# Third exp part of VectorE's pairs multiplied with a scaled copy of V, the second norm in the first norm's buffers, pairs in the first chunk

## The chip, the cores and the metric

One core of a Trainium2 chip runs the whole kernel. Its engines have instruction queues of their own: TensorE (PE, with the loads of its weights as PEld), VectorE (DVE), ScalarE (ACT), GpSimd (POOL) and SyncE (SP), which here only starts DMAs. The metric is the device time of one launch in microseconds, the median of several runs. Beside it stands one execution taken by the hardware profiler; the times of single instructions come from that one.

## The reference

Two identical layers over 2048 rows of 512 values in bf16. Each is an attention block with 32 heads of 16 values, then a dense block with 1792 hidden values and a relu, both behind a norm without weights and with a residual. Both layers use the same weights.

```
x = A_x
x = x + attention(layernorm(x), wqkv, wo)
x = x + relu(layernorm(x) @ w1) @ w2
x = x + attention(layernorm(x), wqkv, wo)
x = x + relu(layernorm(x) @ w1) @ w2

attention: q, k, v = split(x @ wqkv)         # 32 heads of 16
           p = softmax(q @ k.T / 4)           # 2048 x 2048 for each head
           return (p @ v) @ wo
```

The exps of the softmax are the bulk of the work: 2 layers × 32 heads × 2048 × 2048 values.

## The kernel before

**Units, segments, slots.** A unit is the scores of one head for 128 keys (a key block, kb 0 to 15) and 512 query rows. There are 4096 such blocks. A segment (`sg`) is what is summed in one go in `ps_o`: four heads (g 0 to 3, all even or all odd in one group T of eight heads), one chunk of queries (l, j) and a list of key blocks; with all 16 it has 64 units. In layer 1 the queries from row 1024 on are cut in four chunks of 256 rows, and there a unit holds two key blocks of half the width. In the first chunks of a layer segments are split over parts of the key blocks, because K and V are still being made, and their sums are kept in buffers (`acc0`, `acc`) that have other uses later; the eighth of `acc0` is the tile `xn2T`.

The main loop (L1150) runs slot by slot. A slot takes three units, computes their scores into three PSUM banks (L1250; the same matmuls are repeated when PE has time to spare), and takes the exp with one ScalarE activation over 1536 columns (L1259). The products with V (`pv`, L883) follow some slots later; four heads' products run side by side as one round.

**Pairs.** In some slots the third unit goes to VectorE instead, and the activation has only 1024 columns. Two such blocks, taken two slots apart, make a pair. For each block `first_step` (L980) writes `lin`, an integer from which bf16 bits follow that approximate the exp linearly. When the second is there, `chain` (L1015) does five operations over both blocks, 1024 columns: it takes the mantissa out of `lin` (L1020), squares it (L1028), multiplies it by CUBE = 0.1667 (L1029), takes the power of two into `step` (L1020 once more), and multiplies the squared mantissa with `lin` into `cube` (L1032). The exp is the sum of `lin`, `step` and `cube`. Nobody adds them: each of the three is multiplied with V by a matmul of its own, so that a block of a pair costs three products and another block one. V carries two columns of ones, so the softmax's denominators come out of the same products.

**When a pair starts.** The condition at L1173 to L1193 asks that fewer than NP = 4 pairs are under way, that all V of layer 0 is there (`("v", 0, 15) in made`), in layer 1 that K is complete or the pace low, that VectorE's planned work is at most BACKLOG = 6000 ns ahead, and that the pair will be ready before its segment (or one of the next two) ends. NC = 3 buffers exist for `step` and `cube`.

**The order of everything is written out in advance.** The kernel is built by a small planner with clocks of its own for PE and VectorE (`now_pe`, `now_dve`). VectorE's tasks lie in `dve_q` with costs and dependencies; `run_dve` emits those that are due, evacuations of `ps_f` first. PE's other work (projections, transposes, output projection, dense block) lies in `work` as groups of matmuls and is filled in between scores and products, so much for each slot as the pace at L1221 says: what is left, divided by the slots left of the chunk, with some slots added or taken off. `run_until` forces what the next unit needs. So a change of costs or conditions changes the order of all engines' work.

**Norms and buffers.** The first norm of a chunk is transposed into `xnT[j]`, from which Q, K and V are made. The second norm, ahead of the dense block, is transposed into the one tile `xn2T` (L725), which waits (`war_x`) until the H matmuls of an earlier chunk have read it. `h_group` (L653) reads it. At the end of the kernel, L1354 and L1363 use it too.

Of the kernel before, what the change touches and what calls it, by code (L numbers as in the profile page):

```python
# [24 lines left out]
def kernel(  # L25
# [44 lines left out]
    NP = 4  # L70
    NC = 3

    MM = 216.0
# [25 lines left out]
    def sb(shape, dt, name):  # L99
# [11 lines left out]
    kt2 = [sb([P, 2, QS], BF16, f"ktp0_2_{n}") for n in range(2)]  # L111
    kt3 = [sb([P, QS], BF16, f"ktp_{T}_3") for T in range(4)]
    ktp = [
        [[kt01[T][:, 0, :], kt01[T][:, 1, :], kt2[T // 2][:, T % 2, :], kt3[T]] for T in range(4)],
        [
            [sb([P, QS], BF16, f"ktp1_{T}_{j}") for j in range(NQS - 1)] + [kt3[T]]
            for T in range(4)
# [8 lines left out]
        [sb([P, H // 2, PW], BF16, f"vaug1_{kb}") for kb in range(NKB - TPC)] + vaug[0][NKB - TPC :]  # L126
    )
    xnT = [sb([P, NDC, QS], BF16, f"xnT{j}") for j in range(NQS)]
    xn2T = sb([P, NDC, QS], BF16, "xn2T")
    htp = [sb([P, 2, QS], BF16, f"ht{n}") for n in range(NF // 2)]  # L130
# [11 lines left out]
    acc0 = [x[:].bitcast(FP32).rearrange("p a b -> p (a b)") for x in htp]  # L142
    acc0.append(xn2T[:, 0:2, :].bitcast(FP32).rearrange("p a b -> p (a b)"))
    ebuf = [sb([P, W * QS], BF16, f"e{n}") for n in range(NE)]
# [448 lines left out]
    def v_in(b):  # L593
        return b.rearrange("p (h e d) -> p h e d", e=2, d=DH)

    def v_group(l, kb):
        def fin(b):
            nc.vector.tensor_copy(out=v_out(l, kb), in_=v_in(b))
            mark(("v", l, kb))

        return mm_group(v_mms(kb), fin, [("v", l, kb)], each(TPC, "xnT", ("ln1", l, kb // TPC)))
# [51 lines left out]
    def h_group(l, j, ft, war):  # L653
        n = (l * NQS + j) * NF + ft
        _, a, w = columns(l, j)

        number = QS // w
        fts = range(ft, ft + number)
        made_here = [("h", l, j, f) for f in fts]

        def fin(b):
            out = htp[ft // 2][:, ft % 2 : ft % 2 + number, a : a + w]
            sums = b.rearrange("p (f q) -> p f q", f=number)
            if ending[0]:
                nc.scalar.activation(out=out, in_=sums, func=ACTF.Relu)
            else:
                nc.vector.tensor_scalar(  # L667
                    out=out, in0=sums, scalar1=0.0, scalar2=None, op0=ALU.max
                )
            for key in made_here:  # L670
                mark(key)

        def after():
            for f in range(number):
                load_w1(n + f + NW1)

        return mm_group(
            [
                (w1buf[(n + f) % NW1][:, c, :], xn2T[:, c, a : a + w])
                for f in range(number) for c in range(NDC)  # L680
            ],
            fin, made_here,
            each(w // P, "xnT", ("ln2", l, j)) + war + [("w1", n + f) for f in range(number)],
            after=after, wide_by=w, sums=number,
        )
# [32 lines left out]
    def rest_of_chunk(l, j):  # L718
# [4 lines left out]
        war_h = each(chunks[b][1], "z", *b) if b else []  # L723
        war_x = each(NF, "h", *b) if b else []
        work[0:0] = [o_group(l, j, i) for i in range(n)] + ln_groups(  # L725
            ("ln2", l, j), xn2T, a, n, war_x
        )
# [154 lines left out]

    def pv(sg, kb, g, rhs):  # L883
        e = sg["e"]
        sg["rem"][g] -= 1
        nc.tensor.matmul(  # L886
            ps_o[32 * g : 32 * g + 32, 0 : sg["w"]],
            vaug[sg["l"]][kb][:, 4 * sg["T"] + g, 2 * e : 2 * e + 32],
            rhs, start=g not in sg["begun"], stop=not sg["rem"][g],
# [28 lines left out]
    def v_round(found, t):  # L918
        pe_run("v", 1, t)
        sg = segs[seg_at[0]]  # L920
        for n in range(QS // sg["w"]):
            for g in range(4):
                of_g = [f for f in found if f[1][2] == g][n : n + 1]
                for home, x, rhs in of_g:
                    home[:] = [y for y in home if y is not x]
                    pv(sg, x[1], g, rhs)
        while pend and not pend[0]["blocks"]:
# [48 lines left out]
    def dve_block(half, taken, src, ex, recent):  # L976
# [20 lines left out]
        if half == 0:  # L997
            pair_no[0] += 1
            pairs.append({"sg": taken[0][0], "key": ("e", pair_no[0]), "n": pair_no[0], "blocks": [], "mms": []})
# [5 lines left out]
        p["mms"] += [  # L1005
            (sg, kb, g, part[:, half * QS + n * sg["w"] : half * QS + (n + 1) * sg["w"]].bitcast(BF16), key)
            for part, key in (
                (lin[which], line_key), (step[p["n"] % NC], p["key"] + (3,)), (cube[p["n"] % NC], p["key"])
# [6 lines left out]
    def chain(p):  # L1015
# [3 lines left out]
        def bits(keep, put):  # L1019
# [4 lines left out]

        mantissa = stair.bitcast(BF16)
        steps = (
            (342, lambda: bits(0x7F, 0x3F80)),
# [6 lines left out]
        )  # L1034
        for n, (cost, fn) in enumerate(steps):
            k = key + (n,) if n + 1 < len(steps) else key
            early = [("added", p["n"] - NC)] if p["n"] > NC else []
            task(cost, fn, [k], [key + (n - 1,)] if n else early)
            maker[k]["chain"] = p
# [75 lines left out]
    for sg in segs:  # L1115
        both = QS // sg["w"]
        for kbs in zip(*[iter(sg["kbs"])] * both):
            units.extend(tuple((sg, kb, g) for kb in kbs) for g in range(4))
# [17 lines left out]

    wide[0] = False
    seen = set()
    level = 0.0
# [10 lines left out]
    while units:  # L1150
# [15 lines left out]


        half = None
        if len(banked) == W and pair_at in (None, no):
            mine = banked[-1][0][0]  # L1170
            if pair_at == no:
                half, take = 1, pairs[-1]["sg"]
            elif (not pairs or pair_no[0] + 1 - pairs[0]["n"] < NP) and ((mine['l'] or ("v", 0, 15) in made) and (not mine['l'] or ('k', 1, 0, NQS - 1) in made or pace < PAIR_PACE)):  # L1173
                queued = sum(t["cost"] for t in dve_q if "chain" in t)
# [19 lines left out]
            if half is not None:  # L1194
                other = [pairs[-1]["blocks"][0][0][2]] if half else []
                of_take = [x for x in banked if x[0][0] is take]
                if of_take:
                    x = next((x for x in of_take[::-1] if x[0][2] not in other), of_take[-1])
                    banked.remove(x)
                else:  # L1200
                    units.appendleft(banked.pop())
                    x = take_unit(heads(banked) + other, take)
                    for sg, kb, g in x:
                        run_until(("k", sg["l"], sg["T"], kb // TPC))
# [13 lines left out]
        if first["l"] and first["early"]:  # L1218
            rest = sum(x[0][0]["early"] for x in itertools.islice(units, 400)) / W - 20.0
        pace = (  # L1220
            3.0 if first["short"] and not first["l"] else max(todo / max(rest + (0.0 if first["j"] == NQS - 1 and not first["l"] else AHEAD[first["l"]] if first["j"] < (LAST if first["l"] else NQS - 1) else -6.0), 6.0), 0.5)  # L1221
        )
# [194 lines left out]
```

The softmax here doesn't subtract the row's maximum and nothing guards it: scores larger than these inputs give would overflow.

## Time and profile before

| what | value |
|---|---|
| runs shown, median of 8 | 1626.31 us (1624.83 to 1633.44) |
| profiled execution | 1630.59 us |
| its span | 1628.8 us |
| granted TensorE clock, mean | 0.992 |
| score blocks on VectorE | 612 (306 pairs) |
| slots (activations at L1259) | 1366 |

The span is the profiled execution from its first instruction to its last; 1.8 us of its time lie around it. Rows of groups give: line, engine, operation, out <- in, shapes, count, then busy time and mean ns of one, then the idle time of the engine just before them with what ended most of it. The mean is from an instruction's start to its end, and on ScalarE and VectorE one instruction can begin before the one ahead of it has ended. In a list in order of time the first number is the start and the second the length, both in us.

In 40 equal slices of the span, in tenths of the slice, the engines were busy as follows (41 us a slice):

```
PE   8899889999999999999999998889989999999997
DVE  7458999999999999999899999999999999999994
ACT  6999999999999999999999999999999999999994
PEclk9997999999999999999999999999999999999999
```

### The profile page before, as it was taken

To read this page: it belongs to the slowest core of one execution; us is meant where nothing else is said; L and a number is where in the kernel's file an instruction comes from. 1 tells how busy PE (TensorE), PEld (TensorE's weight loads), DVE (VectorE), ACT (ScalarE), POOL (GpSimd) and SP (SyncE) were. 2 spreads that over 40 slices of the span, in tenths; PEclk is the share of its full clock that TensorE was granted. 3 is DMA by queue.
4 is the path that set the end of the run, shared out by engine and by line. 5 is a ranking of instruction groups with operands and counts; after the bars stand their busy time and mean duration, and the time that the engine had idled before them with its cause. 6 is when DMAs were issued, how large, how long until landed. Compare 5 with 4: busy or idle time off the path is not lost.

```text
span 1628.8 us, 35297 instructions
## 1 busy us (share of the span) xinstructions
PE 1491.9 (92%) x14728; PEld 504.7 (31%) x14728; DVE 1507.9 (93%) x3133; ACT 1586.0 (97%) x1385; POOL 96.3 (6%) x279
## 2 busy tenths in 40 slices
PE   8899889999999999999999998889989999999997
PEld 3222222222222222222222222222233333344344
DVE  7458999999999999999899999999999999999994
ACT  6999999999999999999999999999999999999994
POOL 2000001000010010100100000001000110010100
PEclk9997999999999999999999999999999999999999
DMA  5000000210001100111000100000210111112121
GB/s 162 1 1 2 2 2 8 44 28 11 8 15 41 27 14 3 21 41 21 15 1 16 32 1 1 2 3 8 50 26 16 32 27 34 35 39 54 26 61 49
DMA packets 113889, 39.96 MB, mean 25 GB/s; under 512 B 103328, under 2 KB 111264, under 8 KB 113728
## 3 DMA queue, kind: packets, MB, share of 16 engines
q1 hardware_dynamic: 101696, 26.21, 7.0%
q0 software_dynamic: 10688, 10.18, 3.3%
q8 instruction: 115, 1.88, 0.5%
q10 hardware_dynamic: 1344, 1.31, 0.2%
q14 instruction: 46, 0.38, 0.1%
HBM read 24.38 MB, written 2.10 MB: 16 GB/s over the span
## 4 chain that ended last, share of the span: by engine, by line
ACT 81%; PE 9%; DVE 7%; issue 2%; DMA 0%; ACTq 0%; DVEq 0%
ACT e L1259 81%; PE ps_s L1250 3%; PE ps_o L886 2%; PE ps_f L429 2%; DVE lin L980 2%; DVE step L1020 1%; PE ps_s L1313 1%; DVE cube L1032 1%; DVE cube L1028 1%; DVE cube L1029 0%; DVE stats L460 0%; DVE q L610 0%; DVE ht L667 0%; DVE u L809 0%; DVE xn L502 0%
## 5 line engine op out<-in xcount | busy, mean ns | idle before, releaser
L1259 ACT ACTIVATE e<-ps_s 128x1536 bf16<-128x1536 f32 (+1 forms) x1366 | 1576.1, 1403 | 8.4 <-PE ps_s L1250 7.9
L1250 PE MATMUL ps_s<-q,ktp 32*128 32x512 bf16 (+1 forms) x6053 | 603.0, 343 | 91.3 <-ACT e L1259 77.6
L886 PE MATMUL ps_o<-e,vaug 128*32 128x512 bf16 (+1 forms) x4348 | 514.6, 347 | 14.5 <-DVE u L809 5.9
L980 DVE TENSOR_SCALAR lin<-ps_s 128x512 int16<-128x512 f32 x612 | 416.2, 684 | 27.0 <-PE ps_s L1250 22.0
L1250 PEld LDWEIGHTS <-ktp 32*128 32x128 bf16 x6053 | 185.2, 91 | 506.9 <-issue 384.7
L886 PEld LDWEIGHTS <-vaug 128*32 128x32 bf16 x6664 | 166.5, 94 | 349.1 <-issue 337.8
L1020 DVE TENSOR_SCALAR step<-lin 128x1024 int16<-128x1024 int16 x612 | 241.7, 417 | 0.4
L1028 DVE TENSOR_TENSOR cube<-step 128x1024 f16<-128x1024 bf16 x306 | 208.2, 681 | 1.4
L1032 DVE TENSOR_TENSOR cube<-cube,lin 128x1024 bf16<-128x1024 f16 x306 | 207.3, 677 | 0.0
L886 PE MATMUL ps_o<-cube,vaug 128*32 128x512 bf16 (+1 forms) x772 | 147.8, 343 | 0.0
L886 PE MATMUL ps_o<-step,vaug 128*32 128x512 bf16 (+1 forms) x772 | 147.2, 343 | 0.0
L429 PE MATMUL ps_f<-xn2T,w 128*128 128x512 bf16 (+1 forms) x504 | 130.1, 347 | 6.2 <-DVE ht L667 3.3
L886 PE MATMUL ps_o<-lin,vaug 128*32 128x512 bf16 (+1 forms) x772 | 126.6, 340 | 4.3 <-DVE u L809 2.6
L1029 DVE TENSOR_SCALAR cube<-cube 128x1024 f16<-128x1024 f16 x306 | 127.2, 416 | 1.4
L429 PE MATMUL ps_f<-w,ht 128*128 128x512 bf16 x406 | 125.1, 384 | 1.2 <-DVE x L693 0.9
L836 POOL DMA_DIRECT2D r<-u x52 | 38.4, 739 | 1191.7 <-DVE lin L980 605.3
L429 PE MATMUL ps_f<-xnT,wqkv 128*128 128x512 bf16 (+1 forms) x328 | 91.3, 364 | 3.0 <-DVE xnT L553 0.5
L429 PE MATMUL ps_f<-wo,ot 128*128 128x512 bf16 x240 | 74.1, 384 | 1.9 <-DVE x L633 0.7
L610 DVE TENSOR_SCALAR q<-ps_f,qmask 128x512 bf16<-128x512 f32 (+1 forms) x102 | 64.8, 658 | 9.9 <-PE ps_f L429 9.6
L667 DVE TENSOR_SCALAR ht<-ps_f 128x512 bf16<-128x512 f32 x105 | 71.8, 683 | 1.8 <-PE ps_f L429 1.4
L429 PEld LDWEIGHTS <-w 128*128 128x128 bf16 x504 | 39.3, 97 | 64.4 <-issue 55.7
L822 DVE SCALAR_TENSOR_TENSOR ot<-u,mask,r 128x512 bf16<-128x512 f32 (+2 forms) x82 | 51.0, 624 | 1.1
(86 smaller groups left out, 587.4 us busy)
## 6 DMA issues: line engine op xcount, KB each, us to landing
w<-in_B_w_dram SPq DMA_DIRECT2D x140, 128.0 KB
r<-u POOLq DMA_DIRECT2D x25, 256.0 KB, 7.1
r<-u POOLq DMA_DIRECT2D x27, 128.0 KB, 4.6
out_dram<-x SPq DMA_DIRECT2D x16, 128.0 KB
x<-in_A_x_dram SPq DMA_DIRECT2D x14, 128.0 KB
w<-in_B_w_dram SPq DMA_DIRECT2D x1, 1792.0 KB
wqkv<-in_A_wqkv_dram ACTq DMA_DIRECT2D x2, 512.0 KB
c<-u SPq DMA_DIRECT2D x48, 8.0 KB
```

Of the source, the lines that this page charges most:

```text
L429: nc.tensor.matmul(out, lhsT, rhs, start=i % k == 0, stop=i % k == k - 1)
L610: return nc.vector.tensor_scalar(out=qbuf[n % 2][e][:, 0:w], in0=b, scalar1=qmask[e][:, 0:1], scalar2=None, op0=ALU.mult,)
L667: nc.vector.tensor_scalar(out=out, in0=sums, scalar1=0.0, scalar2=None, op0=ALU.max)
L822: nc.vector.scalar_tensor_tensor(out=ot[t][:, at_column + a : at_column + a + w], in0=u[:, a : a + w], scalar=mask[e][:, 0:1], in1=r[:, a ...
L886: nc.tensor.matmul(ps_o[32 * g : 32 * g + 32, 0 : sg["w"]], vaug[sg["l"]][kb][:, 4 * sg["T"] + g, 2 * e : 2 * e + 32], rhs, start=g not in ...
L980: first = nc.vector.tensor_scalar(out=lin[which][:, half * QS : (half + 1) * QS], in0=src, scalar1=EXP_BIAS, scalar2=0.0, op0=ALU.add, op1 ...
L1020: nc.vector.tensor_scalar(out=stair, in0=line, scalar1=keep, scalar2=put, op0=ALU.bitwise_and, op1=ALU.bitwise_or,)
L1028: (609, lambda: nc.vector.tensor_mul(out=power, in0=mantissa, in1=mantissa)),
L1029: (342, lambda: nc.vector.tensor_scalar(out=power, in0=power, scalar1=CUBE, scalar2=None, op0=ALU.mult)),
L1032: (609, lambda: nc.vector.tensor_mul(out=power.bitcast(BF16), in0=power, in1=line.bitcast(BF16))),
L1250: nc.tensor.matmul(b[:, a : a + sg["w"]], kt[32 * g : 32 * g + 32, kc : kc + P], qbuf[sg["n"] % 2][sg["e"]][32 * g : 32 * g + 32, 0 : sg[" ...
L1259: ex = nc.scalar.activation(out=eb[:, 0 : place[m]], in_=b[:, 0 : place[m]], func=ACTF.Exp, scale=1.0 / (LOG2E * UNIT),)
```

## The change

Three things are changed.

1. **A scaled copy of V.** For the key blocks 8 to 11 a second copy of V, `vthird`, holds V times CUBE, the columns of ones included. When both blocks of a pair have such key blocks and the copies are there, the pair leaves out the multiply by CUBE and its `cube` part is multiplied with `vthird`; otherwise it stays as it was. The copies are made on VectorE, once in each layer; in layer 1 they wait for the pairs that still read layer 0's copies. Full segments take these key blocks last, and when a unit is picked for a pair, one with such a key block is looked for in the slot and then further on in the segment.
2. **The second norm goes into the first norm's buffers**: `xnT[j]` in place of `xn2T`, which is gone. The wait `war_x` is gone with it. The eighth of `acc0` is now a tile `kt1`, which holds two tiles of layer 1's K later.
3. **Pairs in the first chunk**, before all V is made: one at a time, from the second K tile of the first group of heads on. And the last chunk of layer 0 plans its other work for 8 slots fewer than it has.

```diff
+    THIRD = (8, 9, 10, 11)
...
+    kt1 = sb([P, 2, QS], BF16, "ktp1_0")
...
-            [sb([P, QS], BF16, f"ktp1_{T}_{j}") for j in range(NQS - 1)] + [kt3[T]]
+            [
+                kt1[:, j, :] if T == 0 and j < 2 else sb([P, QS], BF16, f"ktp1_{T}_{j}")
+                for j in range(NQS - 1)
+            ] + [kt3[T]]
...
+    vthird = {kb: sb([P, H // 2, PW], BF16, f"vthird_{kb}") for kb in THIRD}
-    xn2T = sb([P, NDC, QS], BF16, "xn2T")
...
-    acc0.append(xn2T[:, 0:2, :].bitcast(FP32).rearrange("p a b -> p (a b)"))
+    acc0.append(kt1[:].bitcast(FP32).rearrange("p a b -> p (a b)"))
...
+    def scale_v(l, kb, deps):
+        task(
+            225, lambda: nc.vector.tensor_scalar(
+                out=vthird[kb][:], in0=vaug[l][kb][:], scalar1=CUBE, scalar2=None, op0=ALU.mult
+            ),
+            [("third", l, kb)], [("v", l, kb)] + deps,
+        )
...
     def v_group(l, kb):
         def fin(b):
             nc.vector.tensor_copy(out=v_out(l, kb), in_=v_in(b))
             mark(("v", l, kb))
+            if l == 0 and kb in THIRD:
+                scale_v(l, kb, [])
...
-                (w1buf[(n + f) % NW1][:, c, :], xn2T[:, c, a : a + w])
+                (w1buf[(n + f) % NW1][:, c, :], xnT[xj][:, c, a : a + w])
...
-        war_x = each(NF, "h", *b) if b else []
         work[0:0] = [o_group(l, j, i) for i in range(n)] + ln_groups(
-            ("ln2", l, j), xn2T, a, n, war_x
+            ("ln2", l, j), xnT[xj], a, n, []
         )
...
-    def pv(sg, kb, g, rhs):
+    def pv(sg, kb, g, rhs, p=None):
         e = sg["e"]
+        values = vthird[kb] if p and p["scaled"] else vaug[sg["l"]][kb]
...
-            vaug[sg["l"]][kb][:, 4 * sg["T"] + g, 2 * e : 2 * e + 32],
+            values[:, 4 * sg["T"] + g, 2 * e : 2 * e + 32],
...
+        p["scaled"] = all(
+            ("third", sg["l"], kb) in made for us in p["blocks"] for sg, kb, g in us
+        )
...
-        for n, (cost, fn) in enumerate(steps):
+        nos = (0, 1, 3, 4) if p["scaled"] else range(5)
+        for n, after in zip(nos, (None,) + tuple(nos)):
+            cost, fn = steps[n]
...
-        for kbs in zip(*[iter(sg["kbs"])] * both):
+        order = sorted(sg["kbs"], key=lambda kb: len(sg["kbs"]) == NKB and kb in THIRD)
+        for kbs in zip(*[iter(order)] * both):
...
+        if banked[0][0][0]["l"] and not scaled_two[0]:
+            scaled_two[0] = True
+            for kb in THIRD:
+                scale_v(1, kb, [("added", p["n"]) for p in pairs])
...
-            elif (not pairs or pair_no[0] + 1 - pairs[0]["n"] < NP) and ((mine['l'] or ("v", 0, 15) in made) and (not mine['l'] or ('k', 1, 0, NQS - 1) in made or pace < PAIR_PACE)):
+            elif (not pairs or pair_no[0] + 1 - pairs[0]["n"] < NP) and ((mine['l'] or ("v", 0, 15) in made or not pairs and ("k", 0, 0, 1) in made) and (not mine['l'] or ('k', 1, 0, NQS - 1) in made or pace < PAIR_PACE)):
...
-                if of_take:
-                    x = next((x for x in of_take[::-1] if x[0][2] not in other), of_take[-1])
+                third = half == 0 or all(y[1] in THIRD for y in pairs[-1]["blocks"][0])
+                fit = next(
+                    (
+                        x for x in of_take[::-1]
+                        if third and x[0][2] not in other
+                        and all(("third", y[0]["l"], y[1]) in made for y in x)
+                    ), None
+                )
+                far = None
+                if third and not fit:
+                    far = next(
+                        (
+                            x for x in units if x[0][0] is take
+                            and x[0][2] not in heads(banked[:-1]) + other
+                            and all(
+                                ("third", y[0]["l"], y[1]) in made
+                                and ("k", y[0]["l"], y[0]["T"], y[1] // TPC) in made for y in x
+                            )
+                        ), None
+                    )
+                if far:
+                    units.remove(far)
+                    units.appendleft(banked.pop())
+                    x = far
+                elif fit or of_take:
+                    x = fit or next((x for x in of_take[::-1] if x[0][2] not in other), of_take[-1])
...
-            3.0 if first["short"] and not first["l"] else max(todo / max(rest + (0.0 if first["j"] == NQS - 1 and not first["l"] else AHEAD[first["l"]] if first["j"] < (LAST if first["l"] else NQS - 1) else -6.0), 6.0), 0.5)
+            3.0 if first["short"] and not first["l"] else max(todo / max(rest + (-8.0 if first["j"] == NQS - 1 and not first["l"] else AHEAD[first["l"]] if first["j"] < (LAST if first["l"] else NQS - 1) else -6.0), 6.0), 0.5)
...
-        uses(copy(out=xn2T[:, :, part(i)], in_=pt), more[i], "xnT")
+        uses(copy(out=xnT[NQS - 1][:, :, part(i)], in_=pt), more[i], "xnT")
...
-                    b, w1buf[n % NW1][:, c, :], xn2T[:, c, at_column : at_column + width],
+                    b, w1buf[n % NW1][:, c, :], xnT[NQS - 1][:, c, at_column : at_column + width],
```

More of the change, by code (lines that the diff above doesn't have):

```diff
@@ L654, in h_group @@
         n = (l * NQS + j) * NF + ft
-        _, a, w = columns(l, j)
+        xj, a, w = columns(l, j)
         number = QS // w
@@ L925, in v_round @@
                     home[:] = [y for y in home if y is not x]
-                    pv(sg, x[1], g, rhs)
+                    pv(sg, x[1], g, rhs, *x[5:])
         while pend and not pend[0]["blocks"]:
@@ L998, in dve_block @@
             pair_no[0] += 1
-            pairs.append({"sg": taken[0][0], "key": ("e", pair_no[0]), "n": pair_no[0], "blocks": [], "mms": []})
+            pairs.append({"sg": taken[0][0], "key": ("e", pair_no[0]), "n": pair_no[0], "blocks": [], "mms": [], "scaled": False})
         p = pairs[-1]
@@ L1006, in dve_block @@
             (sg, kb, g, part[:, half * QS + n * sg["w"] : half * QS + (n + 1) * sg["w"]].bitcast(BF16), key)
+            + ((p,) if key == p["key"] else ())
             for part, key in (
@@ L1034, in chain @@
         )
-        for n, (cost, fn) in enumerate(steps):
+        nos = (0, 1, 3, 4) if p["scaled"] else range(5)
+        for n, after in zip(nos, (None,) + tuple(nos)):
+            cost, fn = steps[n]
             k = key + (n,) if n + 1 < len(steps) else key
             early = [("added", p["n"] - NC)] if p["n"] > NC else []
-            task(cost, fn, [k], [key + (n - 1,)] if n else early)
+            task(cost, fn, [k], [key + (after,)] if n else early)
             maker[k]["chain"] = p
@@ L1137 @@
     wide[0] = False
+    scaled_two = [False]
     seen = set()
@@ L1202 @@
                     x = take_unit(heads(banked) + other, take)
+                if True:
                     for sg, kb, g in x:
```

## The prediction

> **What bounds the kernel now.** I read the table of engines first: ACT 97%, DVE 93%, PE 92%. An average names no bound, so the groups by line and shape come next, then engine time by stage, then DVE in order of time.
>
> ```profile
> PE 1491.9 (92%) x14728; PEld 504.7 (31%) x14728; DVE 1507.9 (93%) x3133; ACT 1586.0 (97%) x1385; POOL 96.3 (6%) x279
> ...
> ACT 81%; PE 9%; DVE 7%; issue 2%; DMA 0%; ACTq 0%; DVEq 0%
> ...
> L1259 ACT ACTIVATE e<-ps_s 128x1536 bf16<-128x1536 f32 x753 | 1121.1, 1597 | 4.9 <-PE ps_s L1250 4.6
> L1259 ACT ACTIVATE e<-ps_s 128x1024 bf16<-128x1024 f32 x612 | 673.5, 1164 | 3.5 <-PE ps_s L1250 3.3
> ...
> L1029 DVE TENSOR_SCALAR cube<-cube 128x1024 f16<-128x1024 f16 x306 | 127.2, 416 | 1.4
> ```
>
> ACT waits 8.4 us in all before its exps (4.9 + 3.5) and carries 81% of the chain of waits: the time is the sum of ACT's exps. A slot with a VectorE block has an exp of 1024 columns instead of 1536: 1597 − 1164 = 0.433 us less. So **one block on VectorE takes 0.433 us off the end, a pair 0.866 us.** How many pairs there are (306 now) is a question to VectorE:
>
> ```profile
> 42.00:110.00 68.00, 60.49 (x445) 20.08 (x442) 27.39 (x47) 68.00 (x52) 0.00 (x0) 1.00 0.00 1
> 110.00:161.00 51.00, 47.22 (x337) 12.12 (x336) 43.55 (x86) 47.29 (x42) 0.00 (x0) 0.83 0.01 2
> ...
> 240.00:780.00 540.00, 502.01 (x4126) 153.09 (x4125) 531.43 (x1087) 540.00 (x477) 34.74 (x80) 1.00 0.11 22
> 780.00:830.00 50.00, 45.64 (x376) 14.24 (x373) 44.03 (x92) 49.99 (x44) 4.62 (x13) 1.00 0.05 10
> ...
> 1205.00:1600.00 395.00, 369.01 (x5521) 155.28 (x5521) 379.28 (x818) 393.63 (x343) 33.46 (x75) 1.00 0.16 35
> ```
>
> The columns are PE, PEld, DVE, ACT and POOL busy, granted TensorE clock, DMA. From 240 to 780 DVE is busy 98.4% and ACT 100%: full together. A cheaper pair therefore means more pairs, and more pairs mean less ACT. From 42 to 110 DVE is 40% busy and no pair runs: the first lin is at 111.7.
>
> **Part 1: the third multiply goes (L1029).** Its mean is 416 ns, but DVE's order of time shows what a row occupies:
>
> ```profile
> 836.75 0.69 DVE L980 TENSOR_SCALAR lin<-ps_s 128x512 int16<-128x512 f32 x1
> 837.35 0.42 DVE L1029 TENSOR_SCALAR cube<-cube 128x1024 f16<-128x1024 f16 x1
> 837.68 0.69 DVE L1028 TENSOR_TENSOR cube<-step 128x1024 f16<-128x1024 bf16 x1
> 838.29 0.42 DVE L1020 TENSOR_SCALAR step<-lin 128x1024 int16<-128x1024 int16 x1
> 838.62 0.42 DVE L1029 TENSOR_SCALAR cube<-cube 128x1024 f16<-128x1024 f16 x1
> 838.96 0.68 DVE L1032 TENSOR_TENSOR cube<-cube,lin 128x1024 bf16<-128x1024 f16 x1
> ```
>
> Start to start, L1029 takes 0.335 us, L1020 the same, L980, L1028 and L1032 0.60 each. A pair (two L980, two L1020, L1028, L1029, L1032) occupies 3.41 us, a scaled one 3.07.
>
> Here a rule stands against the row. The Trainium skill ("VectorE: DVE Perf Modes", section "The DRAIN you can't avoid") says that a next operation doesn't start until the pipeline is empty; by that a row frees its whole 0.416 us. The rows overlap by 0.08 us (837.35 + 0.42 is after 837.68), so I count 0.335. By durations the sum below would end at 25 pairs instead of 23, some 2 us lower.
>
> Not all pairs can be scaled: both blocks must have kb 8 to 11. Lin rows by stage, halved, give 28 pairs from 110 to 240, 116 from 240 to 780, 84 from 780 to 1205, 78 after 1205. Full segments hold 16 such blocks and VectorE takes about 10 of 64, so there nearly all scale. Unscaled I count 4 in the first chunk, whose short segments run past kb 11; 6 from 787 to 830, where layer 1 has begun but the copies of V rows 8 to 11 come only at 817 to 827; 12 in the layer-1 segments over kb 12 to 15 (192 of the 1024 units of the first two chunks: 0.19 × 84 = 16, some drawn from a neighbouring segment); and 9, or 3%, where no partner fits. That leaves 275 of 306, estimated between 230 and 300.
>
> Freed: 275 × 0.335 = 92 us. Added: eight scale operations of 128x544. Nearest is L1029 with 1024 columns at 0.335, so they lie between 0.17 and 0.335; I take 0.21, 1.7 us in all. Four of them, in layer 1, wait until the layer-0 pairs under way are added. The order on DVE is written out, so a task whose inputs are not due is not placed; what it can hold up is a pair's scaling, counted above.
>
> What fills the freed 90 us: each further pair costs 3.07, and DVE loses 0.98 × 0.866 = 0.85 us of span by it. **90.3 / 3.92 = 23 pairs, −19.9 us.** With 230 scaled it is 19 pairs (−16.6), with 300 it is 25 (−21.8).
>
> **Part 2: pairs in the first chunk.** K(0,0,1) is copied at 41.5, V(0,15) at 109.7: a window of 68 us in which now one pair at a time may run. From first half to last sum it lives about 10 us: two slots between its halves (68 us hold 52 slots, so 2.6), the chain (2.2 by the pitches, 1.9 scaled), evacuations in between (1 to 2), and the wait for its segment (16 units, 5.3 slots, 7 us long). 68 / 10 gives 6 to 7 pairs, × 0.866 = −5.6 us. DVE has the room: 40.6 us idle against 6.5 × 3.4 = 22. PE hardly has. It waits for ACT 4.3 us there and repeats score matmuls 7 times (177 rows, 156 needed: 1.5 us), 6 us of slack against 5.6 us of shorter slots plus 6.5 × 0.216 = 1.4 us of added PV rounds. So I take −4.5; bounds 0 and −7.
>
> **Part 3: the pace before layer 1 (0 becomes −8).** From 803 to 813 DVE stands idle 5.7 us, for POOL's rstd and for PE's K, Q and xnT groups; lin runs at 0.36 a us from 780 to 830 against 0.43 from 240 to 780. Work done 8 slots earlier can give back at most 3.5 blocks (−1.5 us), and V rows 8 to 11 earlier scale a few pairs more. The same work crowds the slots before it, where PE is 93% busy. I take −1, bounds +2 and −2.5.
>
> **Parts at nothing.** The second norm's transposes no longer wait for the previous chunk's H matmuls; their copy into xn2T had 1.9 us of idle time before it, all for its own transposes, so nothing is released; both bounds are within 1 us. The buffer they now overwrite was read by K, V and Q, all earlier on PE's own queue. ktp1's first two tiles become one with an early life as an accumulator, which ends at 232.7, long before layer 1's K. Later kb 8 to 11 in a segment changes no count. No DMA is added or dropped; the weight loads keep their order on SP's queue.
>
> **Given back.** PE: a pair adds two PV matmuls for each of two blocks, one round of four, 0.216 us, so 30 pairs 6.5 us, and slots shrink 26 us in all. PE waits for ACT 77.6 us over the span and repeats scores besides, but after 1205 it waits only 11.7 us and repeats about 7 us (2230 rows for 2048). With 6 pairs more there it needs 1.3 + 5.2 = 6.5 of 18.7. It fits, not everywhere: I give back 2 us, bounds 0 and 8.
>
> Sum: −19.9 − 4.5 − 1 + 2 = **−23.4**. The profiled execution took 1630.6 around a span of 1628.8; the sum gives 1607.2. The median of the runs is 4.3 lower, 1626.3, which gives **1603**.
>
> **The rivals.**
>
> *PE becomes the bound* where it has least slack (42 to 110, after 1205), 19%. For it: PE is 93% busy after 1205. Against: ACT's waits there are small today. The first window gives nothing, the last 395 us half their share of part 1 (−2.5 of −5), and waits of 2 us more come: −19.9 + 2.5 − 1 + 4 = −14.4, **1612**.
>
> *The freed time isn't used*, 10%: the pair gate counts pairs in flight, a fixed chain allowance of 2500 ns and the units left in a segment, none of which part 1 alters. Against it stands DVE's 98.4%, which shows the backlog as the limit. Only parts 2 and 3 stay, with 2 of slack: about −6, **1620**.
>
> *It is worth more*, 8%: all 306 scale, durations count, the first chunk holds 8 pairs: −23 − 7 − 2.5 = −32.5, **1594**.
>
> *Slower through the clock*, 4%. From 142 to 159 the granted clock is 0.51, PE is the bound, and ACT loses 3.1 us (6.55 of 8 and 7.35 of 9 busy). The Trainium skill ("TensorE: Matmul & The Clock Gate", "HAM oscillation") asks for no PE gap over about 3.4 us. By this rule no dip would come, before or after, and the item is nought; the row has one with no PE wait over 0.9 us, so the rule doesn't exclude more. ACT loses 18% of a half-speed stretch, so 23 us are eaten from 130 us of it on. With 150 us the time is 1603 + 27 = **1630**. Against it: today it is two short stretches, and more pairs mean more needed matmuls. A stretch of the present length more or less is ±3 us.
>
> **How the numbers follow.** The forecast has 59%; its own range, from parts 1 and 2 and the dips, is 1596 to 1610. The range 1592 to 1617 takes in the PE rival and leaves out the unused time, the slower case and the tail of the better one. A measurement of this kernel tells about 0.2% (3.3 us) from nothing. Every case but the clock lies below 1623: faster 0.94, same 0.02, slower 0.04.
>
> **What would show it.** L1029 falls from 306 rows to some 30 to 50, of which about 7 are the new early ones; L980 rises from 612 to about 670; exps of 1024 columns rise by as many, exps of 1536 fall, the slots stay 1366. Lin rows appear between 42 and 110, some 13. DVE stays near 98% from 240 to 780. ACT's waits stay below 12 us. It is wrong if L980 stays near 612, if ACT waits over 20 us for scores, or if more than 80 pairs keep their multiply.

## The result and the profile after

The changed kernel takes **1614.35 us** (median of 11 runs, 1610.96 to 1618.67) against 1626.65 for the kernel before (32 runs, 1623.61 to 1634.27). The ratio is **0.9921**, with an interval of 0.9906 to 0.9936. Run a second time on another occasion it gave 0.9919 (0.9906 to 0.9932). That is 12 us, where 23 were forecast. The time lies in the stated range of 1592 to 1617, near its upper end, and outside the forecast's own 1596 to 1610.

The page of the changed kernel, engines first and then the chain of waits:

```profile
PE 1481.9 (92%) x14863; PEld 509.1 (32%) x14863; DVE 1496.1 (93%) x3007; ACT 1565.5 (97%) x1387; POOL 94.2 (6%) x279
...
ACT 77%; PE 12%; DVE 8%; issue 3%; DMA 1%; ACTq 0%; DVEq 0%
```

ACT lost 4 points of the chain; PE won three. Groups by line and shape of the changed kernel (count | busy us, mean ns | idle before):

```profile
L1311 ACT ACTIVATE e<-ps_s 128x1536 bf16<-128x1536 f32 x703 | 1052.7, 1574 | 3.4 <-PE ps_s L1302 1.7 <-PE ps_o L901 1.2
L1311 ACT ACTIVATE e<-ps_s 128x1024 bf16<-128x1024 f32 x662 | 718.2, 1149 | 1.4 <-PE ps_s L1302 1.2 <-PE ps_o L901 0.2
...
L1048 DVE TENSOR_SCALAR cube<-cube 128x1024 f16<-128x1024 f16 x24 | 10.0, 417 | 0.2
```

The short exps rose from 612 to 662: 50 more blocks are on VectorE, in 331 pairs, and only 24 pairs keep the multiply (L1048, which was L1029). Engine time by stage of the changed kernel:

```profile
42.00:110.00 68.00, 60.62 (x470) 20.11 (x467) 45.60 (x84) 68.00 (x55) 0.00 (x0) 1.00 0.00 1
...
240.00:780.00 540.00, 506.57 (x4198) 153.42 (x4198) 529.65 (x1036) 538.57 (x482) 32.58 (x80) 1.00 0.11 22
...
830.00:1080.00 250.00, 228.59 (x1946) 70.97 (x1943) 232.30 (x454) 249.41 (x219) 7.48 (x24) 1.00 0.04 9
```

From 240 to 780 VectorE is as full as before (98.1%) with fewer instructions: the freed time went into pairs. From 830 to 1080 it is at 92.9%, where it had been at 96.7%:

```profile
830.00:1080.00 250.00, 228.03 (x1935) 69.29 (x1937) 241.68 (x487) 249.27 (x218) 6.81 (x24) 1.00 0.04 9
```

There the room was not used (102 lin rows against 100). Why not is open; 13 of the 24 pairs that keep the multiply lie there.

So the blocks came. Where did their gain go? The list of ACT in order of time tells: from the first exp to the last, how much of it ACT waited (waits over 0.15 us), and what lies behind the last exp. For all kernels of this study, each from its own profiled execution (us). The last two columns are of all runs and are explained below the table:

| kernel | blocks | exps | ACT's waits between them | behind the last exp | span | clock of the runs | at full clock |
|---|---|---|---|---|---|---|---|
| before | 612 | 1576.6 | 7.5 | 28.0 | 1628.8 | 0.995 | 0 |
| changed | 662 | 1554.8 | 3.9 | 35.1 | 1610.7 | 0.996 | −12.4 |
| changed, again (e12) | 662 | 1556.1 | 7.2 | 35.3 | 1615.3 | 0.997 | −12.3 |
| e1 no scaling | 616 | 1574.5 | 3.7 | 29.0 | 1623.9 | 0.997 | −0.5 |
| e2 scaling only | 654 | 1558.7 | 11.7 | 35.0 | 1622.1 | 0.995 | −2.4 |
| e3 multiply dropped | 612 | 1576.4 | 8.5 | 28.1 | 1629.7 | 0.997 | −0.1 |
| e4 hurry | 666 | 1559.6 | 11.3 | 29.3 | 1616.9 | 0.997 | −5.6 |
| e5 pace of before | 664 | 1554.3 | 10.7 | 33.7 | 1615.3 | 0.997 | −6.6 |
| e6 no early pairs | 656 | 1559.3 | 11.2 | 36.7 | 1624.0 | 0.995 | −6.9 |
| e7 stop at 64 | 654 | 1558.4 | 3.9 | 28.3 | 1607.3 | 0.997 | −14.2 |
| e8 no repeats | 660 | 1555.8 | 7.2 | 29.9 | 1609.7 | 0.997 | −12.4 |
| e9 early only | 616 | 1574.2 | 4.0 | 28.1 | 1624.3 | 0.997 | −1.2 |
| e10 buffers only | 612 | 1576.3 | 8.3 | 30.0 | 1631.3 | 0.989 | +2.8 |
| e11 stop at 64, pace 10 | 656 | 1558.2 | 8.0 | 30.2 | 1613.0 | 0.996 | −10.4 |

The first exp begins at 16.6 to 18.0 in all of them, so with it the columns add up to the span. From before to changed: exps −21.8 (50 × 0.433 is 21.7), waits −3.6, **behind the last exp +7.1**, and 0.2 for the first exp's later start, together −18.1.

Three of these terms hold stretches of low TensorE clock, which fall elsewhere in each execution. In the profile of before ACT waits 4.7 us in two of them (3.4 from 142 to 161, 1.3 from 1126 to 1134). In that of the changed kernel one lies behind the last exp, from 1592.0 to 1595.5 at a clock of 0.51. The same eight matmuls there, and before:

```profile
1592.15 1.86 PE L1365 MATMUL ps_s<-xnT,w 128*128 128x256 bf16 x8 [0.18 <-DVE xnT L1406]
...
1611.75 1.03 PE L1313 MATMUL ps_s<-xn2T,w 128*128 128x256 bf16 x8 [0.18 <-DVE xn2T L1354]
```

From the start of this closing work (L1365, before it was L1313) to the end the changed kernel takes 28.9 us, before 27.5, and e5, whose closing work met no low clock, 27.5 (1587.8 to 1615.3). So of the 7.1 us **5.7 are leftover work and 1.4 are low clock**. (The ends of e1, e2, e4, e10, e11 and e12 met low clock too, for 1 to 2.3 us each.) Without the low clock's 4.7 and 1.4 the difference is −14.8. In before's exps stand 2.7 us more of it (an estimate: 17 exps there that waited, at 0.14 us each, see e4, and 0.36 us of shorter waits), which leaves −12.1, where the medians say −12.3.

**The last two columns.** Each run has a mean granted clock, and within each kernel its time follows it: 27 runs of before in one series go from 1624.5 us at 1.000 to 1637.1 at 0.986. One slope fitted to all 255 runs is 0.93 us for each 0.001, with a scatter of 0.6 us. "At full clock" is an estimate from this line at 1.000, less before's 1623.5, good to 0.3 to 0.6 us. It compares orders of instructions as if none had met low clock; whether an order brings low clock about is another question.

What PE does behind the last exp of the changed kernel, which ends at 1575.6:

```profile
1575.65 0.38 PE L901 MATMUL ps_o<-e,vaug 128*32 128x256 bf16 x4
1575.96 1.05 PE L434 MATMUL ps_f<-xnT,w 128*128 128x256 bf16 x8
1576.84 1.04 PE L434 MATMUL ps_s<-xnT,w 128*128 128x256 bf16 x8
1577.71 3.19 PE L434 MATMUL ps_s<-w,ht 128*128 128x512 bf16 x14
1581.75 0.38 PE L1365 MATMUL ps_s<-x,ident 128*128 128x512 bf16 x1 [0.85 <-DVE x L708]
```

Two H groups and a whole Z group (14 matmuls) of the last chunk but one are done only here, and take 5.8 us before the closing work (L1365) begins. Before, whose last exp ends at 1600.8, no such group is left, and the closing work follows the last products at once:

```profile
1601.33 0.39 PE L1313 MATMUL ps_s<-x,ident 128*128 128x512 bf16 x1
```

PE's other work had not got done in the shorter slots.

### The profile page after: what moved, and what is told of

Read it like the earlier page. It is cut to its first block, busy times and chain, and to the rows that moved or that the text cites. A ratio compares the mean times of both kernels' runs of the same rounds, so it can differ in the third digit from the quotient of the medians.

```text
span 1610.7 us, 35448 instructions
## 1 busy us (share of the span) xinstructions
PE 1481.9 (92%) x14863; PEld 509.1 (32%) x14863; DVE 1496.1 (93%) x3007; ACT 1565.5 (97%) x1387; POOL 94.2 (6%) x279
## 4 chain that ended last, share of the span: by engine, by line
ACT 77%; PE 12%; DVE 8%; issue 3%; DMA 1%; ACTq 0%; DVEq 0%
ACT e L1311 77%; PE ps_s L1302 4%; PE ps_f L434 4%; PE ps_o L901 3%; DVE lin L995 2%; DVE step L1036 1%; PE ps_s L1365 1%; DVE cube L1047 1%; DVE cube L1051 1%; DVE stats L465 0%; DVE ot L836 0%; DVE ht L682 0%; DVE q L625 0%; DVE x L708 0%; DMA c<-u 0%
## 5 line engine op out<-in xcount | busy, mean ns | idle before, releaser
L1311 ACT ACTIVATE e<-ps_s 128x1024 bf16<-128x1024 f32 (+1 forms) x1366 | 1554.3, 1368 | 4.8 <-PE ps_s L1302 2.9
L1302 PE MATMUL ps_s<-q,ktp 32*128 32x512 bf16 (+1 forms) x6060 | 599.6, 340 | 91.6 <-ACT e L1311 75.0
L901 PE MATMUL ps_o<-e,vaug 128*32 128x512 bf16 (+1 forms) x4284 | 494.1, 345 | 10.3 <-DVE u L823 4.8
L995 DVE TENSOR_SCALAR lin<-ps_s 128x512 int16<-128x512 f32 x662 | 450.9, 684 | 34.0 <-PE ps_s L1302 28.5
L1302 PEld LDWEIGHTS <-ktp 32*128 32x128 bf16 x6060 | 189.6, 91 | 504.0 <-issue 375.8
L1036 DVE TENSOR_SCALAR step<-lin 128x1024 int16<-128x1024 int16 x662 | 261.3, 417 | 3.3 <-PE ps_o L901 0.6
L1047 DVE TENSOR_TENSOR cube<-step 128x1024 f16<-128x1024 bf16 x331 | 224.8, 682 | 2.7
L1051 DVE TENSOR_TENSOR cube<-cube,lin 128x1024 bf16<-128x1024 f16 x331 | 224.2, 678 | 0.0
L901 PE MATMUL ps_o<-cube,vthird 128*32 128x512 bf16 (+1 forms) x788 | 137.9, 337 | 0.0
L434 PE MATMUL ps_f<-xnT,w 128*128 128x512 bf16 (+1 forms) x496 | 126.8, 349 | 2.3 <-DVE ht L682 1.1
L434 PE MATMUL ps_f<-w,ht 128*128 128x512 bf16 x392 | 119.7, 384 | 0.9 <-DVE q L625 0.3
L901 PEld LDWEIGHTS <-vthird 128*32 128x32 bf16 x788 | 39.8, 95 | 32.8 <-issue 30.1
```

Of the source, the lines that this page charges most:

```text
L434: nc.tensor.matmul(out, lhsT, rhs, start=i % k == 0, stop=i % k == k - 1)
L901: nc.tensor.matmul(ps_o[32 * g : 32 * g + 32, 0 : sg["w"]], values[:, 4 * sg["T"] + g, 2 * e : 2 * e + 32], rhs, start=g not in sg["begun" ...
L995: first = nc.vector.tensor_scalar(out=lin[which][:, half * QS : (half + 1) * QS], in0=src, scalar1=EXP_BIAS, scalar2=0.0, op0=ALU.add, op1 ...
L1036: nc.vector.tensor_scalar(out=stair, in0=line, scalar1=keep, scalar2=put, op0=ALU.bitwise_and, op1=ALU.bitwise_or,)
L1047: (609, lambda: nc.vector.tensor_mul(out=power, in0=mantissa, in1=mantissa)),
L1051: (609, lambda: nc.vector.tensor_mul(out=power.bitcast(BF16), in0=power, in1=line.bitcast(BF16))),
```

## The experiments

Ratios are to the kernel before in the same series, with their intervals; medians are of all runs of the series.

**e1: every pair keeps its multiply.**

```diff
-        p["scaled"] = all(...)
+        p["scaled"] = False
```

> The changed kernel with every pair keeping its multiply by CUBE (no vthird, no scaling operations); early pairs, pace and norm buffers stay. The program has 308 pairs against 331. Theory (the gain is the freed VectorE time turned into pairs): 4 blocks fewer on ACT than before, -1.7 us, end as short as before: about 1624, ratio 0.998 to 1.000. Rival (early pairs and pace carry the gain): near the changed kernel's 1614, ratio 0.993. L1048 back to 308 rows, DVE busy over 97% from 240 to 780.

1625.84 us, ratio 0.9997 (0.9988 to 1.0005), at full clock −0.5. Early pairs and pace without the scaling bring next to nothing; the rival falls.

**e2: scaling without early pairs, with the pace of before.**

```diff
-... or ("v", 0, 15) in made or not pairs and ("k", 0, 0, 1) in made ...
+... or ("v", 0, 15) in made ...
-... max(todo / max(rest + (-8.0 if ...
+... max(todo / max(rest + (0.0 if ...
```

> The changed kernel without the early pairs and with the pace of before: part 1 alone (and the norm buffers). The program has 327 pairs, and 24 512-column matmuls more behind the last exp than before. Theory: 42 blocks fewer on ACT, -18.2, end longer by 5.2 to 7: about 1615, ratio 0.993. Rival (early pairs are worth their 4.5 us): 1619, ratio 0.995.

1624.63 us, ratio 0.9994 (0.9981 to 1.0008): **nothing**, against 1615 and 1619, and at full clock no more than −2.4. Both theories missed it. The blocks came off ACT (1558.7), but the end has its 7 us more (about 1.5 of them low clock) and ACT waits 11.7. ACT in order of time, e2:

```profile
786.22 32.60 ACT L1311 ACTIVATE e<-ps_s 128x1536 bf16<-128x1536 f32 x28 [0.38 <-PE ps_s L1302]
821.16 2.47 ACT L1311 ACTIVATE e<-ps_s 128x1536 bf16<-128x1536 f32 x2 [2.34 <-PE ps_s L1302]
...
857.63 152.11 ACT L1311 ACTIVATE e<-ps_s 128x1536 bf16<-128x1536 f32 x134 [2.64 <-PE ps_s L1302]
```

The number in brackets is ACT's wait in front of the line: 2.3 us for scores at 819, 2.6 at 855; between 780 and 1080 they sum to 8.5. PE is then in `wo` and K groups that the next units need (`run_until`), and the scores (L1302) queue behind them:

```profile
817.53 1.46 PE L434 MATMUL ps_f<-wo,ot 128*128 128x512 bf16 x6 [0.16 <-issue]
819.77 1.02 PE L434 MATMUL ps_f<-wqkv,xnT 128*128 128x512 bf16 x4 [0.78 <-DVE x L648]
820.73 0.39 PE L1302 MATMUL ps_s<-q,ktp 32*128 32x512 bf16 x3
```

The same stretch of the changed kernel holds one line:

```profile
779.01 217.63 ACT L1311 ACTIVATE e<-ps_s 128x1024 bf16<-128x1024 f32 x190 [0.38 <-PE ps_s L1302]
```

**e3: the multiply dropped, the pairs not increased.** In the kernel before:

```diff
-            (342, lambda: nc.vector.tensor_scalar(
-                out=power, in0=power, scalar1=CUBE, scalar2=None, op0=ALU.mult)),
+            (342, lambda: None),
```

> The kernel before, in its own order, with the multiply by CUBE planned but not issued (the factor is left out of the cube part, so the output differs); the 306 pairs and all slots stay as they were. Theory (VectorE's freed time is worth nothing until more blocks move to it; ACT sets the end): within 0.2% of before, ratio 0.998 to 1.000, DVE busy down by 306 x 0.335 = 102 us if the row occupies its pitch, by 127 us if it occupies its duration. Rival (VectorE's own pace already delays the end): 5 us or more faster, ratio 0.997 or less.

1625.71 us, ratio 0.9993 (0.9983 to 1.0003), at full clock −0.1: freed VectorE time as such is worth nothing. Its busy time fell by 81 us, neither by 102 nor by 127. VectorE's first row, before and in e3:

```profile
L980 DVE TENSOR_SCALAR lin<-ps_s 128x512 int16<-128x512 f32 x612 | 416.2, 684 | 27.0 <-PE ps_s L1250 22.0
...
L980 DVE TENSOR_SCALAR lin<-ps_s 128x512 int16<-128x512 f32 x612 | 419.3, 688 | 77.6 <-PE ps_s L1249 72.3 <-issue 0.2
```

The idle time in front of it rose from 27.0 to 77.6. The lengths of all VectorE rows together (count × mean) fell by 119 us, the 127 of the dropped rows less 9 by which the others got longer, and 37 us of overlap between neighbours went with them. Of these, 25 belong to the dropped rows themselves (306 × 0.081, as the forecast's 0.335 has it). The other 12 go with idle time: 716 rows now stand after some, where 496 did, and such a row overlaps nothing. So a pitch tells what a row frees only while the engine stays full.

**e4: PE may overrun.**

```diff
-            else 3.0 if not first["l"] and first["j"] == NQS - 1 else 99.0
+            else 3.0 if not first["l"] and first["j"] == NQS - 1 else 2.0 if first["l"] and first["j"] >= 2 else 99.0
```

> The changed kernel with one number altered: in layer 1's chunks of 256 rows PE's other work may go 1 us past its limit when the pace is over 2.0 (it was 99). The program has 333 pairs, and as many matmul columns behind the last exp as the kernel before (53504 against 52480; the changed kernel 64768). Theory (7 us of the gain are given back behind the last exp, because PE's other work of the last chunk isn't done): span from the last exp to the end back to 28 to 29 us from 35, 54 blocks fewer than before: about 1605, ratio 0.987. Rival (PE has no room after 1205, and work pulled forward stalls ACT): ACT waits over 8 us more for scores there, time 1613 or more.

1622.09 us, ratio 0.9969 (0.9958 to 0.998). The end is short (29.3), as the theory says, and the time worse than the changed kernel's, as the rival says. Groups of e4:

```profile
L1311 ACT ACTIVATE e<-ps_s 128x1536 bf16<-128x1536 f32 x699 | 1043.6, 1566 | 8.6 <-PE ps_s L1302 6.2 <-PE ps_o L901 1.2 <-DVE cube L1051 0.4
L1311 ACT ACTIVATE e<-ps_s 128x1024 bf16<-128x1024 f32 x666 | 718.5, 1141 | 4.4 <-PE ps_s L1302 3.8 <-PE ps_o L901 0.2
```

ACT waits 7.8 us after 1205, in pieces of at most 0.5, and its exps take 1559.6 where 54 blocks fewer would give 1576.6 − 23.4 = 1553.2. So 6 us more are lost than the waits show. ACT's starts tell why. Without a wait they lie 1.331 us apart for long exps and 0.905 for short ones (medians in before and in e4), while a lone exp lasts 1.45 and 1.02: the exps overlap by some 0.12 us. One that waits loses this besides its wait, 0.14 us in the mean. In e4 61 exps waited for any length of time, in before 25: 36 × 0.14 is 5 us, and waits too short to be counted add 0.8. So PE, with the repeats of its score matmuls, had no free room for the work behind the last exp.

**e5: pace of before; e6: no early pairs.** Each takes back one of the two edits of e2.

> The changed kernel with the pace of before in the last chunk of layer 0 (0 slots in place of 8 fewer); scaled and early pairs stay. The program has 332 pairs and the same end behind the last exp as the changed kernel. Theory (with more pairs the slots of that chunk are too short for PE's other work; what isn't done by layer 1's start stalls ACT, as in the run without early pairs and pace, where ACT waited 2.3, 0.5 and 2.6 us at 819, 831 and 855): ACT waits 6 to 9 us between 780 and 1080, about 1622, ratio 0.997. Rival (the pace is worth the 1 us of the prediction, and the lack of early pairs cost the run before its gain): about 1615, ratio 0.993.

1619.8 us, ratio 0.9949 (0.993 to 0.9968). ACT waits 8.1 us between 780 and 1080, the changed kernel 0.5. The stall is the pace's, as the theory says; the time is between the two expectations, at full clock 5.8 us behind the changed kernel.

> The changed kernel without pairs before V is complete; scaled pairs and the pace of 8 slots fewer stay. The program has 328 pairs and 8 512-column matmuls more behind the last exp than the changed kernel. Theory (pace decides, early pairs are worth their blocks): 6 blocks more on ACT, +2.6, end +1.7: about 1618.5, ratio 0.995. Rival (early pairs carry the gain): 1622 or more, ratio 0.997 or more.

1621.7 us, ratio 0.9958 (0.9945 to 0.9971): the microseconds are 3 above the theory, the ratio holds the theory's 0.995. At full clock it is 5.5 us behind the changed kernel, where the theory's terms make 4.3. The six blocks are 2.6 of it. The leftover work takes 8.9 us from the last exp to the closing work in place of 6.2, with 32 H matmuls in place of 16, which is 2.7. So early pairs are worth their blocks and as much again at the end. The waits are 7 longer in this execution, but 6.7 of its 11.2 lie in low-clock stretches.

**e7: no new pair in the last 64 units.**

```diff
-        if len(banked) == W and pair_at in (None, no):
+        if len(banked) == W and (pair_at == no or pair_at is None and len(units) >= 64):
```

> The changed kernel, but no new pair starts when fewer than 64 units are left. The program has 327 pairs, 8 blocks fewer on VectorE than the changed kernel, and 22 512-column matmuls fewer behind the last exp (53504 columns against 64768; before 52480). Theory (the end is long because the last chunk's pairs shorten the slots in which PE does its other work): +3.5 for the blocks, -4.8 to -7 for the end: about 1611 to 1613, ratio 0.990 to 0.992; last exp to end 28 to 30 us. Rival (the end is long for another reason, so the matmuls only move): last exp to end stays at 34 to 35 us, 1618.

1613.53 us, ratio 0.9904 (0.9884 to 0.9924): as the theory expected. Eight blocks go back to ACT, and the end shrinks from 35.1 (33.7 without its low clock) to 28.3. ACT in order of time, e7, at the end:

```profile
1559.55 19.48 ACT L1311 ACTIVATE e<-ps_s 128x1536 bf16<-128x1536 f32 x15
1584.13 1.08 ACT L1375 CAST x<-ps_s 128x512 bf16<-128x512 f32 x2 [5.11 <-PE ps_s L1365]
```

The relus that the changed kernel has between these two lines (L680, the late H groups) are gone. **This shows that pairs at the end made the end long**: the last four of them brought 3.5 us and cost 5.4. Against the changed kernel the ratios' intervals overlap (0.9921 and 0.9919). At full clock e7 is 1.7 us faster (±0.6), which is what 5.4 − 3.5 says; it rests on six runs and on the fitted line.

**e8: no repeated score matmuls in the last four chunks.**

```diff
-        short = FLOOR * 1330.0 - level - busy[0] - MM * (1 + soon)
+        short = (0.0 if first["l"] and first["j"] >= 2 else FLOOR) * 1330.0 - level - busy[0] - MM * (1 + soon)
```

> The changed kernel without repeated score matmuls in layer 1's chunks of 256 rows (the repeats fill PE's spare time; the program has 246 score matmuls fewer). It has 330 pairs and 13 512-column matmuls fewer behind the last exp than the changed kernel. Theory (PE has little room there; what it repeats is missing for other work): +0.9 for 2 blocks, -2.8 to -4 for the end: about 1611.5, ratio 0.990. Rival (the repeats keep PE's clock up): granted clock below 0.97 after 1205 and 1618 or more.

1614.24 us, ratio 0.9916 (0.9897 to 0.9935). The end is 5.2 shorter (3.8 without the low clock), so the repeats did stand in the way of PE's other work; ACT waits 3.3 more and the exps take 1.0 more, and no gain is left. The clock stayed up (0.999, and 1.00 after 1205): the rival falls.

**e9: early pairs only; e10: buffers only.** e1 with the pace of before, and the same without early pairs.

> The changed kernel with the early pairs alone: every pair keeps its multiply and the pace is that of before. The program has 308 pairs (616 blocks). Two things are asked. Whether early pairs alone move the time: theory -1.7 us for 4 blocks, ratio 0.998 to 1.000; rival (they carry the gain) 0.995 or less. And whether they keep TensorE's clock up: so far the profiles with early pairs have mean clocks of 0.997 to 1.000, those without 0.991 to 0.996; theory here 0.997 or more and a spread of the runs under 5 us (before: 10).

1624.86 us, ratio 0.9979 (0.9968 to 0.9989): 3.7 us below before in the same series, of 1.7 expected; at full clock 1.2. The profile's clock was 0.996 and the runs spread over 6.6 us, both outside what was expected if early pairs keep the clock up. The runs leave it open: e9's mean clock is 0.997 against 0.995 of before beside it, and every kernel with early pairs has 0.996 or 0.997, those without 0.989 to 0.996, but e3, which has none, has 0.997.

> The changed kernel with the norm buffers alone: every pair keeps its multiply, no early pairs, pace of before. The program has 306 pairs and as many slots as before. Theory: the buffers are worth nothing, ratio 0.998 to 1.002. Rival (the wait for the earlier chunk's H matmuls held up PE's other work): 3 us or more faster, ratio 0.998 or less. If early pairs keep the clock up, the clock here is 0.991 to 0.996 and the spread of the runs 7 us or more.

1635.08 us, ratio **1.0056** (1.0039 to 1.0074): slower, which neither expected. In its profile the end is 2.0 longer than before's, and at 1204 ACT waits 2.6 us. VectorE in order of time, e10:

```profile
1203.63 0.25 DVE L847 RECIPROCAL c<-c 128x16 f32<-128x16 f32 x1 [2.08 <-DMA c<-u]
1203.80 0.63 DVE L1049 TENSOR_TENSOR cube<-cube,lin 128x1024 bf16<-128x1024 f16 x1
```

The planner placed a reciprocal ahead of its DMA's landing; VectorE stood 2.1 us, the `cube` behind it was late, PE waited 1.7 us for it, and ACT for PE. Such an accident belongs to this order, not to the buffers. At full clock the order costs 2.8 us, and this wait is most of it; the longer end is a stretch of low clock (0.50 from 1599.6 to 1606.4). The rest of the 6.6 us between the medians goes with the clock: e10's six runs have a mean of 0.989, the 27 of before beside them 0.995. Whether this order brings low clock about, six runs can't say.

**e11, e12: stop at 64 with a pace of 10; the changed kernel again.**

> No new pair below 64 units left, and 10 slots in place of 8 before layer 1. The program has 328 pairs and 51456 matmul columns behind the last exp (4 512-column matmuls fewer than with 64 units alone). Theory (blocks, waits and end add up): -0.9 for 2 blocks and -0.9 for the end against the run with 64 units alone, if ACT's waits between 780 and 1205 stay near 2 us: 1609 to 1612, ratio 0.989 to 0.990. Rival (the order shifts enough to bring new waits there): 1615 or more.

1615.7 us, ratio 0.9936 (0.9923 to 0.9949). The end is 30.2 (over 2 us of it low clock), but ACT waits 8.0, of it 3.9 between 1080 and 1205 (2.5 in one piece at 1181, the rest under low clock): the rival's new waits. Two more blocks and four matmuls fewer at the end than in e7 turned into a slower kernel, by 3.8 us at full clock.

> The changed kernel as it is, beside the two runs with a stop, on the same chip: ratio 0.992 as at first, and last exp to end 35 us. If the stop at 64 units is worth its 3.5 - 7 = -3.5 us, this one is 2 to 5 us slower than the run with 64 units and a pace of 10.

1613.91 us, ratio 0.9919 as at first, and 35.3 behind the last exp. That it would be slower than e11 didn't come true.

## Why the prediction was right in direction and short in size

**Right.** ACT sets the end, and VectorE's time counts only through blocks: e3 shows it. A block is worth about 0.43 us: by starts that don't wait it is 1.331 − 0.905 = 0.426, and the exps shrank by 21.8 for 50 blocks. That this is 0.433 each to the digit is partly luck, since before's exps hold low clock. Forecast were 30 pairs more, 25 came: 5 early pairs from 42 to 110 (10 lin rows) where 6.5 were taken, and some 20 by the freed time in place of 23. Pairs that keep the multiply: 24, fewer than the 30 to 50 named. VectorE stayed at 98% from 240 to 780, and ACT's waits below 12 us.

**The step that failed** is "Given back": "It fits, not everywhere: I give back 2 us, bounds 0 and 8." Leftover work measured 5.7, within the bounds and nearly three times the size. The sum there set PE's slack over all 395 us after 1205 (18.7 us) against what pairs need (6.5). That is an average. The work of the last chunks has no later slots to slide into, and its lack shows behind the last exp and not as ACT's waits, which is where the prediction looked. Put in what was measured, −21.8 for −24.4 of the blocks, 5.7 for 2, and nothing for part 3, and −23.4 becomes −16. Then 2.7 of the −21.8 are before's low clock, and ACT's waits outside low clock rose by 1.1 (2.8 to 3.9). That makes −12.3, as the medians say.

**Part 3 was mis-sized.** "I take −1, bounds +2 and −2.5" valued the pace by the idle time that it would give back in the order of before. In the order with more pairs its lack costs 8 us of stalls (e2, e5), in e5 5.8 us of time. The forecast counted pairs and pace as terms to be added. They aren't: scaling alone 0.9994, early pairs and pace alone 0.9997, all of it 0.9921 (at full clock −2.4, −0.5 and −12.4). More pairs shorten the slots in which PE's other work is due, and the pace moves that work forward; each needs the other.

**"Parts at nothing"** held the buffers within 1 us. The missing wait may be worth nothing, but the order that the planner builds with these buffers alone was 0.56% slower, 2.8 us of it at full clock.

**The rivals.** "PE becomes the bound" (1612) came nearest, in time and in the resource; its place was only half right, since the first window stalled nowhere. "The freed time isn't used" holds for 830 to 1080 alone; its sum of about −6 for what would stay was too good, since e1, which keeps all of that, has −0.5. The clock did not make it slower, but the rival's price for it was too low: ACT was to lose 18% of a half-speed stretch, and by the slope over the runs it is about 29% (an estimate: 0.93 us lost for each 0.001 of 1625 us, halved).

**The range.** That it holds the result is in part luck. It was drawn to take in the PE rival, and with the pace left as it was, a part priced at 1 us, the time would have been 1620 (e5), outside it.

**The overlap of VectorE's rows.** The prediction sets the Trainium skill ("VectorE: DVE Perf Modes", section "The DRAIN you can't avoid") against its row. The same section adds that a next operation which is not held starts earlier, so the page leaves room for the row's 0.08 us of overlap; 0.335 was the right count while VectorE is full.

## What to carry to other kernels

When the bound engine gets shorter stages, ask of every engine that works in its shadow how much work it must finish by which stage; a mean slack says nothing of the last stage, where leftover work falls behind the end. When a planner orders everything, parts of a change can't be priced one by one: run each alone and all together. And an edit of a few matmuls can move such a kernel by several us through the new order, so single variants within 0.3% of each other prove little. Where the clock differs between runs, compare variants at the same clock before you explain a difference.

## What the runs showed of the hardware

TensorE's clock fell to about half in all profiles but e7's, in one to five stretches each, at places that differ between two executions of one kernel (changed: 1592; again: 235, 597, 1580). They last 3.5, 6.9, 10.3 or 17.2 us, whole multiples of 3.45. Before's two (0.50 from 142.3 to 159.4, 0.51 from 1125.3 to 1132.2) came with PE 85 and 88% busy in the 10 us ahead and no PE wait above 0.62 us in the 15 us ahead. In four of the 29 stretches a PE wait of 1.8 to 3.4 us lay ahead, in the others none above 1.1 us. Here it is in e6, by stages of 10 us (the third number from the right is the clock):

```profile
980.00:990.00 10.00, 9.32 (x64) 2.80 (x63) 8.54 (x18) 8.40 (x7) 0.00 (x0) 0.69 0.00 0
...
1120.00:1130.00 10.00, 9.18 (x69) 2.17 (x62) 7.90 (x17) 8.28 (x8) 2.20 (x9) 0.69 0.00 0
```

By the slope over the runs (an estimate) a stretch of 3.5 us costs 1 us and one of 17 us 5. The two profiles of the changed kernel differ in this way: 3.9 us of waits at a mean clock of 0.998, 7.2 us at 0.994. What sets it off stays open.
